# Banded and strided attention into a SoLU layer: local units of five and four blocks, masks seeded by ScalarE, w_out prepared with GpSimd and TensorE, and a new instruction order

## The chip, the cores and the metric

The kernel runs on one core of one Trainium2 chip, in one launch. The time is the device time of a whole execution in microseconds (us). The host only lays the data out.

## The reference

Eight batches, eight heads, 576 positions, head dimension 64. Four heads attend locally (a position sees itself and the 31 before it), four attend with stride 32 (the earlier positions with the same residue). Their outputs, side by side, are 4608 tokens of 512 values, which go through a SoLU layer with a layer norm.

```python
rel = pos[:, None] - pos[None, :]
mask_local = (rel >= 0) & (rel < 32)
mask_strided = (rel >= 0) & (pos[None, :] % 32 == pos[:, None] % 32)
attn = softmax(where(mask, q @ k.T / sqrt(64), -1e9)) @ v      # 4 local heads, 4 strided heads
x = attn_out.transpose(0, 2, 1, 3).reshape(4608, 512)
h = x @ w_in                                                   # 512 -> 1024
solu = h * softmax(h)
ln = (solu - mean(solu)) / sqrt(var(solu) + 1e-6) * g_ln
out = ln @ w_out                                               # 1024 -> 512
```

The two weight matrices come as 64-bit floats, everything else as 32-bit floats.

## The kernel before, in words

**Precision by pairs.** The large products run in float16 with each operand as a high and a low part: hi = cast(x), lo = x - hi, and three matmuls hi*hi, hi*lo, lo*hi. ScalarE (ACT) makes hi, VectorE (DVE) makes lo. Before that the weights and v are scaled by a power of two that comes of their sum of squares (`pow2_scale`). QK runs in float32.

**Weights.** `decode` loads a quarter of w_in or w_out (128 x 1024 numbers of 64 bits), lets ScalarE turn the high words into float32 values (L603), and VectorE shift the low words (L606) and OR their top three bits in (L607). w_in is decoded into `cc_sb`, and TensorE's Gram matmuls (L620) give its sum of squares; `whi`, `wlo` (the tile `w`) are its halves. w_out is decoded into `obuf`; eight ScalarE squares (L639) give its column sums, weighted by g; `ohi` (L651) and `olo` (in `obuf`, L652) are its halves, scaled by g and the power of two (`gs`). The raw words lie in "rooms": pieces of `raw_sb`, and once the buffers of two c transposes. `raw_sb` also holds the working tiles of the SoLU layer and a second v buffer, so that a room is free only when the work in it is done. The last quarter of w_out uses the room of an earlier one.

**Attention units.** A batch is cut into five units, `UNITS`: strided with 6 and 5 blocks, local with 3, 3 and 3. `unit(n)` issues for each: the mask into the score bank `s_ps` (by identity matmuls L369 for the first six units, later as a ScalarE copy L361, called a seed), the QK matmuls on top (L374), the row maximum (L380), the exponentials, either one per block with the maximum as bias (L385, units in `BY_BLOCK`) or a VectorE subtraction and one large exponential (L390, L392), sums and reciprocals, the multiply by the reciprocal on GpSimd (L401, POOL), the halves of p (L409, L410), one DMA transpose p to pt (L412), the PV matmuls into the banks `x_ps` (L432 strided, L442 local), and the copies of x as halves into the rings `xl`, `xs` (L461, L462). The local v is also needed shifted by half a tile: three DMAs copy it into `ve` (L338).

**Token blocks.** `ff(n)` does one of 36 blocks of 128 tokens: two times 12 large matmuls, called g1 here (L505 to L507), into two of three banks `h_ps`; the maximum (L511), the exponentials (L515), h times e (L517), the centring (L521), the square pass (L522), the powers on GpSimd, the halves of the result c (L562, L563), one DMA transpose of 16 tiles, cc to cc (L566), two times 12 large matmuls, called g2 (L575 to L577), into `o_ps`, and the scaled store (L583) with its DMA from ScalarE's queue.

**Order.** `Plan.add` records each step with its engine, a duration and its reads and writes; `ORDER` is a list of step numbers, and the program is issued in that order. Each engine works through its own steps in order. SP issues all loads and transposes from one queue, in order.

Of the kernel before, what the change touches and what calls it, by code (L numbers as in the profile page):

```python
# [753 lines left out]
```

## Time and profile before

| | us |
|---|---|
| median of three runs | 501.76 (500.56 to 502.09) |
| profiled execution | 501.38 |
| its span, first to last instruction | 499.7 |
| TensorE busy in the span | 462.6 (93%) |
| ScalarE / VectorE / GpSimd busy | 363.3 / 352.0 / 159.8 |
| mean granted TensorE clock | 0.952 |

A profile line names engine, operation, output and input tiles; "idle before" is the time in which the engine had nothing to do just before an instruction, with what ended it. PE is TensorE's matmul side and PEld its weight loads, which overlap. A clock of 0.5 is half of TensorE's full speed. The DMA share is the mean share of time in which a DMA engine was at work, added up over packets, so it can pass 1. In 40 slices of the span TensorE reads:

```profile
PE   6441889999999999999999999999999999999996
```

### The profile page before, as it was taken

How to read it: one execution, taken by the hardware profiler on the slowest of the kernel's cores; microseconds unless marked ns; L12 is line 12 of the kernel's file. 1: busy time of each engine (PE TensorE's matmuls, PEld its weight loads, DVE VectorE, ACT ScalarE, POOL GpSimd, SP SyncE). 2: the span in 40 equal slices, each digit the busy share in tenths (PEclk: the TensorE clock that was granted, in tenths of full speed). 3: DMA queues.
4: the chain of work that ended last, by engine and by line, in shares of the span. 5: the costliest groups of instructions: out<-in, count | busy, mean ns of one | idle time of the engine just before them, and what ended most of it. 6: DMA issues, size and time to landing. Idle time of an engine off the chain costs nothing.

```text
span 499.7 us, 12461 instructions
## 1 busy us (share of the span) xinstructions
PE 462.6 (93%) x5049; PEld 241.4 (48%) x5049; DVE 352.0 (70%) x740; ACT 363.3 (73%) x647; POOL 159.8 (32%) x312
## 2 busy tenths in 40 slices
PE   6441889999999999999999999999999999999996
PEld 5341544455455555555555545454555544444442
DVE  2988879678788777787877778578868664543440
ACT  3796899998687777888859667966857558455741
POOL 3210131662336163253442303450543304023220
PEclk8555889999999999999999999999999999999999
DMA  8999968599897599769969999449376465643343
GB/s 330 336 326 261 353 187 163 158 189 184 187 207 180 133 259 257 131 173 231 213 145 197 254 185 175 84 90 218 85 138 121 78 123 101 132 102 74 84 97 106
DMA packets 153818, 88.03 MB, mean 176 GB/s; under 512 B 139808, under 2 KB 140448, under 8 KB 153248
## 3 DMA queue, kind: packets, MB, share of 16 engines
q1 hardware_dynamic: 148576, 77.79, 69.8%
q10 hardware_dynamic: 5184, 9.44, 5.6%
q8 instruction: 39, 0.64, 0.5%
q14 instruction: 19, 0.16, 0.1%
HBM read 39.24 MB, written 9.44 MB: 97 GB/s over the span
## 4 chain that ended last, share of the span: by engine, by line
PE 80%; DMA 13%; ACT 3%; SPq 2%; DVE 1%; issue 1%; ACTq 0%; DVEq 0%
PE h_ps L505 11%; PE o_ps L575 11%; PE h_ps L507 11%; PE h_ps L506 11%; PE o_ps L576 11%; PE o_ps L577 11%; PE s_ps L374 6%; DMA raw<-w_in 4%; DMA cc<-cc 3%; DMA raw<-w_out 3%; PE x_ps L442 3%; DMA pt<-p 3%; PE x_ps L432 2%; DMA q<-qstr 1%; ACT t L385 1%
## 5 line engine op out<-in xcount | busy, mean ns | idle before, releaser
L575 PE MATMUL o_ps<-ohi,cc 128*128 128x512 f16 x272 | 103.3, 380 | 0.2
L577 PE MATMUL o_ps<-ohi,cc 128*128 128x512 f16 x272 | 103.1, 379 | 0.0
L576 PE MATMUL o_ps<-obuf,cc 128*128 128x512 f16 x272 | 103.1, 379 | 0.0
L401 POOL TENSOR_TENSOR t<-t,m 128x576 f32<-128x576 f32 (+2 forms) x40 | 48.5, 1214 | 117.3 <-DVE m L398 93.8
L511 DVE TENSOR_REDUCE st<-h_ps 128x1 f32<-128x512 f32 x70 | 47.3, 681 | 32.6 <-PE h_ps L507 32.3
L563 DVE SCALAR_TENSOR_TENSOR cc<-raw,st,cc 128x1024 f16<-128x1024 f32 (+1 forms) x38 | 46.6, 1229 | 23.5 <-ACT cc L562 23.1
L515 ACT ACTIVATE raw<-h_ps,st,vsc 128x512 f32<-128x512 f32 x62 | 47.8, 773 | 19.7 <-DVE st L513 18.8
L505 PE MATMUL h_ps<-w,xl 128*128 128x512 f16 x140 | 53.7, 384 | 1.8 <-DVE raw L517 1.8
L517 DVE SCALAR_TENSOR_TENSOR raw<-h_ps,raw 128x512 f32<-128x512 f32 x70 | 47.1, 683 | 11.7 <-ACT raw L515 11.2
L374 PE MATMUL s_ps<-k,q 64*54 64x54 f32 (+1 forms) x1280 | 45.6, 284 | 9.1 <-ACT s_ps L361 7.4
L507 PE MATMUL h_ps<-w,xl 128*128 128x512 f16 x140 | 53.6, 383 | 0.0
L506 PE MATMUL h_ps<-w,xl 128*128 128x512 f16 x140 | 53.6, 383 | 0.0
L505 PE MATMUL h_ps<-w,xs 128*128 128x512 f16 x140 | 53.5, 382 | 0.0
L521 ACT ACTIVATE raw<-raw,st 128x1024 f32<-128x1024 f32 x36 | 41.3, 1147 | 16.8 <-DVE st L520 15.8
L506 PE MATMUL h_ps<-w,xs 128*128 128x512 f16 x140 | 53.3, 381 | 0.0
L507 PE MATMUL h_ps<-w,xs 128*128 128x512 f16 x140 | 53.3, 381 | 0.0
L562 ACT ACTIVATE cc<-raw,st 128x1024 f16<-128x1024 f32 (+1 forms) x38 | 41.5, 1100 | 13.9 <-POOL st L552 9.6
L374 PEld LDWEIGHTS s_ps<-k,q 64*54 64x54 f32 (+1 forms) x1280 | 40.0, 201 | 19.8 <-ACT s_ps L361 8.8
L380 DVE TENSOR_REDUCE m<-s_ps 128x6 f32<-128x576 f32 (+2 forms) x40 | 30.4, 760 | 25.7 <-PE s_ps L374 25.2
L577 PEld LDWEIGHTS <-cc 128*128 128x128 f16 x288 | 28.2, 98 | 34.5 <-DMA cc<-cc 0.6
L575 PEld LDWEIGHTS <-cc 128*128 128x128 f16 x288 | 28.1, 98 | 33.4 <-DMA cc<-cc 1.0
L576 PEld LDWEIGHTS <-cc 128*128 128x128 f16 x288 | 28.2, 98 | 31.5
(149 smaller groups left out, 828.4 us busy)
## 6 DMA issues: line engine op xcount, KB each, us to landing
out<-ob ACTq DMA_DIRECT2D x36, 256.0 KB, 2.4
k<-kstr SPq DMA_DIRECT2D x8, 594.0 KB, 5.4
q<-qstr SPq DMA_DIRECT2D x8, 594.0 KB, 5.5
k<-kloc SPq DMA_DIRECT2D x8, 576.0 KB, 5.7
q<-qloc SPq DMA_DIRECT2D x8, 576.0 KB, 6.4
raw<-w_in SPq DMA_DIRECT2D x4, 1024.0 KB, 15.6
vrs<-vstr SPq DMA_DIRECT2D x5, 768.0 KB, 7.6
vrl<-vloc SPq DMA_DIRECT2D x5, 640.0 KB, 6.5
```

Of the source, the lines that this page charges most:

```text
L374: nc.tensor.matmul(s_ps[row : row + nq, pair, i * nk : (i + 1) * nk], q_raw[half][hs, q0 : q0 + (nq - 1) * nqb + 1 : nqb], k_raw[half][hs, ...
L401: add("pool", nx * nk / 520 + 0.03, lambda: nc.gpsimd.tensor_tensor(tv, tv, sm.unsqueeze(2).broadcast_to([P, nx, nk]), op=ALU.mult), r=TM, ...
L505: nc.tensor.matmul(hv[i], xhi[cc], whi[:, cc, cols], start=(cc == 0), stop=False)
L506: nc.tensor.matmul(hv[i], xhi[cc], wlo[:, cc, cols], start=False, stop=False)
L507: nc.tensor.matmul(hv[i], xlo[cc], whi[:, cc, cols], start=False, stop=(cc == 3))
L511: add("dve", 0.69, lambda i=i: nc.vector.tensor_reduce((nm, nm2)[i], hv[i], axis=AX.X, op=ALU.max, negate=True), r=[HH[i]], w=[(ST, "nm", i)])
L515: add("act", 0.73, lambda i=i, q=q: nc.scalar.activation(e[:, parts2[i]], hv[i], AF.Exp, bias=nm, scale=hs, accum_out=q), r=[HH[i], (ST, " ...
L517: add("dve", 0.7, lambda i=i, x=x: nc.vector.scalar_tensor_tensor(u[:, parts2[i]], hv[i], 1.0, e[:, parts2[i]], op0=ALU.mult, op1=ALU.mult ...
L563: add("dve", w / 980 + 0.23, lambda cols=cols: nc.vector.scalar_tensor_tensor(c[:, 1, cols], u[:, cols], r, c[:, 0, cols], op0=ALU.mult, o ...
L575: nc.tensor.matmul(o, ct[:, cc, :], ohi[:, cc, :], start=(cc == 0), stop=False)
L576: nc.tensor.matmul(o, ct[:, cc, :], olo[:, cc, :], start=False, stop=False)
L577: nc.tensor.matmul(o, ct[:, 8 + cc, :], ohi[:, cc, :], start=False, stop=(cc == 7))
```

## The change

- **Units.** `LATER` cuts batches 1 to 7 into four units: strided 6 and 5, local 5 and 4. Batch 0 keeps five. A local unit of more than four blocks puts its two head pairs in the two x banks, and its copies of x are two; one of four blocks or fewer uses one bank. The tiles t, p and pt are now bound to the unit's place in the batch, with transposes of 20 and 16 tiles.
- **Masks.** All units are seeded by ScalarE; the strided mask is read straight from the loaded masks. To make that possible TensorE's warm-up matmuls write the score banks once.
- **Weights.** The low word's top bits are taken by GpSimd from the highest byte of each low word, (byte - 15.5)/32 written as an integer; VectorE keeps only the OR. The squares of w_out are Gram matmuls; the scale is made of the sum of squares of w_out times that of g.
- **v.** The scrap output of v's squares goes into a buffer of vs instead of one of its own.
- **Order.** `ORDER` is another list throughout.

```diff
-BY_BLOCK = (2, 3, 4, 7, 8, 9)
+LATER = [(1, 0, 6), (1, 6, 5), (0, 0, 5), (0, 5, 4)]
+BY_BLOCK = (2, 3, 4, 7, 8)
 ORDER = """
-1 5 7 2 0 6 8 11 10 13 12 15 14 17 9 21 3 25 4 29 53 45 54 55 68 56 46 57 69 47 58 70 59 48 71 49 88 60 72 83 73 61 51 74 89 62 90 84 18 91 52 22 100
+1 6 2 15 3 16 4 14 11 13 19 20 25 18 53 30 52 54 17 35 60 12 55 56 10 58 5 61 144 92 59 21 22 62 123 63 9 76 23 64 77 27 65 24 66 78 67 79 93 97 80 68
 ...
-    def warm():
-        for _ in range(40):
-            nc.tensor.matmul(o_ps[:, 0:P], ones, ones, start=True, stop=True)
+    def warm(n, out):
+        for i in range(n):
+            nc.tensor.matmul(out[i % len(out)], ones, ones[:, 0:1].broadcast_to([P, 5 * KL]), start=True, stop=True)
 ...
     # unit(n)
-        half, b0, nb = UNITS[j]
+        half, b0, nb = (LATER if b else UNITS)[j]
-        if n >= SEEDED:
-            def seed():
-                nc.scalar.copy(s_ps[:, :, 0 : nb * nk], mk.unsqueeze(1).broadcast_to([P, 2, nb * nk]))
-            add("act", nx * nk / 1200 + 0.17, seed, r=["mask"], w=[("s", 0), ("s", 1)])
+        add("act", nx * nk / 1200 + 0.17, lambda: nc.scalar.copy(sv, mk), r=[MK], w=[("s", 0), ("s", 1)])
-            for pair, h, hs, row in heads if n < SEEDED else ():
-                nc.tensor.matmul(s_ps[row : row + D, pair, 0 : nb * nk], unit_sb[hs, hs], mk[hs], start=True, stop=False)
-        nt = 12
+        nt = 12 if half else 2 * nx
-        X = [("x", xb)] if half == 0 else [("x", 0), ("x", 1)]
+        one = half == 0 and nb <= 4
+        X = [("x", xb)] if one else [("x", 0), ("x", 1)]
 ...
     # v_scale(b)
-                nc.scalar.activation(junk[:, 0 : VW[a]], vr_sb[raw][a], AF.Square, scale=2.0**-SQ, accum_out=vm[:, a : a + 1])
+                nc.scalar.activation(junk[:, a, 0 : VW[a]], vr_sb[raw][a], AF.Square, scale=2.0**-SQ, accum_out=vm[:, a : a + 1])
 ...
     # decode
-            nc.vector.tensor_scalar(w0, w0, 29, None, op0=ALU.logical_shift_right)
-            nc.vector.scalar_tensor_tensor(di, di, 3, w0, op0=ALU.logical_shift_left, op1=ALU.bitwise_or)
+        top = raw.bitcast(U8).rearrange("p f (t b) -> p f t b", b=4)[:, :, 0, 3]
+        add("pool", 1.05, lambda: nc.gpsimd.tensor_scalar(w0, top, -15.5, 1.0 / 32, op0=ALU.add, op1=ALU.mult), r=RAW, w=[("low", n)])
+        add("dve", 1.25, lambda: nc.vector.scalar_tensor_tensor(di, di, 3, w0, op0=ALU.logical_shift_left, op1=ALU.bitwise_or),
 ...
     # prep_o
-            for cc in (2 * i, 2 * i + 1):
-                add("act", 0.71, lambda cc=cc: nc.scalar.activation(ob_sb[cc % 2][:, 0 : DM // 2].bitcast(BF16), obuf[:, cc], AF.Square,
-                                                                   scale=2.0**-SQ, accum_out=o_sc[:, 8 + cc : 9 + cc]),
+            def gram(i=i, dst=dst):
+                x = dst.bitcast(BF16).rearrange("p (f t) -> p f t", t=2)[:, :, 1]
+                for j in range(8):
+                    nc.tensor.matmul(o_ps[:, 0:P], x[:, j * P : j * P + P], x[:, j * P : j * P + P], start=(i == 0 and j == 0), stop=(i == 3 and j == 7))
+            add("pe", 0.6, gram, r=OD, w=["o"])
```

The order moves everywhere; three places show what. The names are those of the tiles above, with a buffer number.

SP's queue around the loads of w_out, before (two quarters have the room `raw`, one the room in `cc`; the last of the four is the third `raw<-w_out`):

```order
L285 DMA raw_67<-w_out 128x2x1024
L412 DMA_TRANSPOSE pt_98<-p_94 128x12x128
L338 DMA ve_74<-vl_71 32x2x1024
L338 DMA ve_74<-vl_71 64x2560
L285 DMA raw_67<-w_out 128x2x1024
L661 DMA g_118<-g 128x8
L412 DMA_TRANSPOSE pt_97<-p_96 128x12x128
L285 DMA cc_103<-w_out 128x2x1024
L285 DMA k_65<-kloc 128x1152
L285 DMA raw_67<-w_out 128x2x1024
L285 DMA q_63<-qloc 128x1152
```

The same place now:

```order
L288 DMA raw_67<-w_out 128x2x1024
L411 DMA_TRANSPOSE pt_97<-p_95 128x12x128
L288 DMA k_66<-kstr 128x1188
L342 DMA ve_73<-vl_70 64x2560
L288 DMA raw_67<-w_out 128x2x1024
L288 DMA cc_102<-w_out 128x2x1024
L411 DMA_TRANSPOSE pt_96<-p_94 128x12x128
L288 DMA raw_67<-w_out 128x2x1024
L288 DMA k_65<-kloc 128x1152
L288 DMA q_63<-qloc 128x1152
```

The last quarter now stands ahead of both local loads of batch 1; the strided k of batch 1 and one copy into ve stand ahead of the second quarter.

ScalarE from the decode of the last quarter to the first square pass of a token block, before (L639 are the squares of w_out, L515 the exponentials of block 0, L325 the split of the next v):

```order
L603 ACTIVATE obuf_114<-raw_67 128x1024
L639 ACTIVATE ob_105,o_sc_117<-obuf_114 128x512
L409 CAST p_96<-t_86 128x12x54
L392 ACTIVATE t_87<-t_87 128x540
L639 ACTIVATE ob_104,o_sc_117<-obuf_114 128x512
L639 ACTIVATE ob_105,o_sc_117<-obuf_114 128x512
L639 ACTIVATE ob_104,o_sc_117<-obuf_114 128x512
L515 ACTIVATE raw_67,st_106<-h_ps,st_106,vsc_77 128x512
L461 CAST xl_99<-x_ps 128x2x192
L515 ACTIVATE raw_67,st_106<-h_ps,st_106,vsc_77 128x512
L325 ACTIVATE vl_71<-vrl_69,vsc_78 128x1280
L409 CAST p_94<-t_87 128x2x5x54
```

The same place now, to the centring (the square pass L520 comes next):

```order
L601 ACTIVATE obuf_113<-raw_67 128x1024
L408 CAST p_94<-t_85 128x6x96
L364 CAST s_ps<-mk_loc_81 128x2x480
L391 ACTIVATE t_84<-t_84 128x540
L408 CAST p_92<-t_83 128x12x54
L384 ACTIVATE t_85,m_89<-s_ps,m_89 128x96 x10
L459 CAST xl_98<-x_ps 128x2x192
L513 ACTIVATE raw_67,st_105<-h_ps,st_105,vsc_76 128x512 x2
L652 ACTIVATE ohi_109<-obuf_113,gs_118 128x512 x2
L408 CAST p_93<-t_84 128x2x5x54
L519 ACTIVATE raw_67<-raw_67,st_105 128x1024
```

The squares are gone, the v split comes later, and the ten block exponentials of the first five-block unit stand ahead of the exponentials of block 0.

TensorE at the first output-layer matmul, before (84 of the g1 matmuls stand ahead of it, and the QK of a local unit directly):

```order
L507 LDWEIGHTS xs_102
L507 MATMUL h_ps<-w_113,xs_102 128x512
L374 MATMUL s_ps<-k_65,q_63 64x96 x12
L575 LDWEIGHTS cc_103
L575 MATMUL o_ps<-ohi_110,cc_103 128x512
```

And now:

```order
L505 MATMUL h_ps<-w_112,xs_101 128x512
L263 LDWEIGHTS ones_111
L263 MATMUL s_ps<-vm_74,ones_111 128x1
L263 LDWEIGHTS ones_111
L263 MATMUL s_ps<-vm_74,ones_111 128x1
L573 LDWEIGHTS cc_102
L573 MATMUL o_ps<-ohi_109,cc_102 128x512
```

Again 84 g1 matmuls stand ahead (a float32 QK matmul counts twice in the profile); the QK of the four-block unit and one PV of 60 matmuls of batch 1 now come behind.

More of the change, by code (lines that the diff above doesn't have):

```diff
@@ L262, in total @@
             for i, part in enumerate(parts):
-                nc.tensor.matmul(tot, ones, part.bitcast(BF16)[:, 1:2], start=(i == 0 and not adds), stop=(i == len(parts) - 1), skip_group_check=adds)
+                one = product or not (i or adds)
+                nc.tensor.matmul(tot[:, i : i + 1] if product else tot, ones, part.bitcast(BF16)[:, 1:2], start=one, stop=product or i == len(parts) - 1, skip_group_check=adds)
         add("pe", 0.06 * len(parts) + 0.05, total, r=["ones", *r], w=[T])
         def root():
-            nc.vector.tensor_scalar(dst[:, 0:1].bitcast(I32), tot.bitcast(I32), 1, 0x7F800000, op0=ALU.logical_shift_right, op1=ALU.bitwise_and)
+            low = tot
+            if product:
+                low = dst[:, 0:1]
+                nc.vector.tensor_scalar(low, tot[:, 0:1], tot[:, 1:2], None, op0=ALU.mult)
+            nc.vector.tensor_scalar(dst[:, 0:1].bitcast(I32), low.bitcast(I32), 1, 0x7F800000, op0=ALU.logical_shift_right, op1=ALU.bitwise_and)
         def fn():
@@ L300, in v_scale @@
         raw = raw_v(b)
+        junk = v_sb[1][b % 2]
         for a in range(2):
             def square(a=a):
-                nc.scalar.activation(junk[:, 0 : VW[a]], vr_sb[raw][a], AF.Square, scale=2.0**-SQ, accum_out=vm[:, a : a + 1])
-            add("act", (1.36, 1.58)[a], square, r=[("vr", a, raw)], w=["junk", ("vm", b % 2, a)])
+                nc.scalar.activation(junk[:, a, 0 : VW[a]], vr_sb[raw][a], AF.Square, scale=2.0**-SQ, accum_out=vm[:, a : a + 1])
+            add("act", (1.36, 1.58)[a], square, r=[("vr", a, raw)], w=[("v", 1, b % 2, a), ("vm", b % 2, a)])
         room = (s_ps[:, 1, 512 - b : 513 - b], ("s", 1)) if b else (h_ps[2][:, 0:1], ("h", 2))
-        pow2_scale(sc, [vm[:, 0:1], vm[:, 1:2]], [("vm", b % 2, a) for a in range(2)], ("vsc", b % 4), room, 8, 1.0 / P_SCALE, adds=b > 1)
+        pow2_scale(sc, [vm[:, 0:1], vm[:, 1:2]], [("vm", b % 2, a) for a in range(2)], ("vsc", b % 4), room, 8, 1.0 / P_SCALE, adds=b > 0)
         def hscale():
@@ L374, in qk @@
                     nc.tensor.matmul(s_ps[row : row + nq, pair, i * nk : (i + 1) * nk], q_raw[half][hs, q0 : q0 + (nq - 1) * nqb + 1 : nqb],
-                                     k_raw[half][hs, k0 : k0 + nk], start=False, stop=(i == nb - 1), skip_group_check=n >= SEEDED)
-        add("pe", nb * 0.231 + (0.25, 0.09)[half] - (0.2 if n >= SEEDED else 0.0), qk, r=[("q", half), ("k", half), "mask", "unit", "kpad"], w=[("s", 0), ("s", 1)])
+                                     k_raw[half][hs, k0 : k0 + nk], start=False, stop=(i == nb - 1), skip_group_check=True)
+        add("pe", nb * 0.231 + (0.25, 0.09)[half] - 0.2, qk, r=[("q", half), ("k", half), "kpad"], w=[("s", 0), ("s", 1)])
         SS = [("s", 0), ("s", 1)]
@@ L404, in unit @@
         if half == 0:
-            hi, lo = (pb[:, 6 * a : 6 * a + 6, 0:nk] for a in range(2))
+            hi, lo = (pb[:, nx * a : nx * a + nx, 0:nk] for a in range(2))
         else:
@@ L449, in unit @@
             q0, w = off + QL * b0, QL * nb
-            src = [x_ps[xb][:, 0 : 2 * w].rearrange("p (c q) -> p c q", c=2)]
-            dst = [[x[:, :, q0 : q0 + w] for x in xl]]
+            src = [x_ps[xb][:, 0 : 2 * w].rearrange("p (c q) -> p c q", c=2)] if one else [x[:, 0:w] for x in x_ps]
+            dst = [[x[:, :, q0 : q0 + w] for x in xl]] if one else [[x[:, c, q0 : q0 + w] for x in xl] for c in range(2)]
             ring = [("xl", q0 // QL + i) for i in range(nb)]
@@ L458, in unit @@
         for c, (src, (dh, dl)) in enumerate(zip(src, dst)):
-            w = 2 * by_row[c] * nq if half else nx * nq
-            K = [(*x, c) if half else x for x in ring]
+            w = 2 * by_row[c] * nq if half else (2 if one else 1) * nb * nq
+            K = [(*x, y) for x in ring for y in (range(2) if one else (c,))]
             add("act", w / 1200 + 0.17, lambda src=src, dh=dh: nc.scalar.copy(dh, src), r=[X[c]], w=[(*x, "h") for x in K])
@@ L479, in ff @@
         bs = sorted({n * P // S, (n * P + P - 1) // S})
-        ring = [("xl", pos // QL + i, a) for i in range(2) for a in "hl"]
+        ring = [("xl", pos // QL + i, c, a) for i in range(2) for c in range(2) for a in "hl"]
         ring += [("xs", b % 2, b0, c, a) for b in bs for b0 in R0 for c in range(2) for a in "hl"]
@@ L673, in attn_solu_kernel @@
         v_split(b, 0)
-        for j in range(2, NU - 1):
+        last = len(LATER if b else UNITS) - 1
+        for j in range(2, last):
             unit(b * NU + j)
@@ L681, in attn_solu_kernel @@
                 o_factor(b + 1)
-        unit(b * NU + NU - 1)
+        unit(b * NU + last)
         if b == 0:
```

85 lines of the change are left out of this document (41 added, 44 removed), and 82 rows, old and new, of the table ORDER.

## The prediction

> **What bounds the kernel now.** I read the page's totals and clock row, then busy time by stretches of the span, then the chain of waits around the stretch that is not full, then ScalarE and TensorE there in order of time.
>
> ```profile
> PE 462.6 (93%) x5049; PEld 241.4 (48%) x5049; DVE 352.0 (70%) x740; ACT 363.3 (73%) x647; POOL 159.8 (32%) x312
> PEclk8555889999999999999999999999999999999999
> ...
> 22.00:53.00 31.00, 13.32 (x360) 11.58 (x361) 26.92 (x51) 22.99 (x53) 4.06 (x4) 0.50 1.10 286
> 53.00:82.00 29.00, 24.91 (x309) 12.32 (x308) 24.93 (x53) 27.09 (x62) 4.83 (x5) 0.93 0.86 228
> ...
> 0.00:82.00 82.00, 49.38 (x862) 33.21 (x863) 64.38 (x127) 63.51 (x137) 15.48 (x26) 0.71 0.97 287
> 82.00:475.00 393.00, 392.30 (x4097) 199.06 (x4094) 282.14 (x603) 291.92 (x498) 141.25 (x277) 1.00 0.74 158
> 475.00:499.70 24.70, 20.91 (x97) 9.12 (x94) 5.48 (x12) 7.89 (x13) 3.09 (x9) 1.00 0.41 101
> ```
>
> The columns are the length, then busy time of PE, PEld, DVE, ACT, POOL, then clock and DMA share. From 82 to 475 us TensorE idles 393.00 - 392.30 = 0.70 us: nothing another engine saves there is worth more. It idles 3.79 us at the end and 32.62 us before 82, where its clock is 0.71 on average. So the time is "when the queue of TensorE fills" plus the work behind that point. I anchor on the first output-layer matmul (L575): 84 first-layer matmuls (g1) stand ahead of it in the old order, and 84 in the new.
>
> ```profile
> 26.58 2.03 ACT t L385 x12
> ...
> 40.73 6.84 DMA raw<-w_out
> ...
> 48.81 1.23 DVE obuf L607
> 50.07 7.03 DMA raw<-w_out
> ```
>
> This is the chain of waits: the second quarter of w_out lands at 47.57 and is decoded, its OR ends at 50.04, that frees the room for the last quarter, which is issued at 50.07 and lands at 57.10. ScalarE, which had idled 4.43 us for the second quarter, then runs without a pause:
>
> ```profile
> 47.60 1.19 ACT L603 ACTIVATE obuf<-raw 128x1024 f32<-128x1024 f32 x1 [4.43 <-DMA raw<-w_out]
> ...
> 52.35 0.68 ACT L409 CAST p<-t 128x576 f16<-128x576 f32 x1
> 52.92 0.63 ACT L639 ACTIVATE ob<-obuf 128x512 bf16<-128x512 f32 x1
> ...
> 55.56 0.64 ACT L361 CAST s_ps<-mk_loc 128x576 f32<-128x576 bf16 x1
> 57.12 1.20 ACT L603 ACTIVATE obuf<-raw 128x1024 f32<-128x1024 f32 x1 [0.93 <-DMA raw<-w_out]
> ...
> 60.60 0.63 ACT L639 ACTIVATE ob<-obuf 128x512 bf16<-128x512 f32 x1
> ...
> 61.21 0.62 ACT L639 ACTIVATE ob<-obuf 128x512 bf16<-128x512 f32 x1
> ...
> 63.76 1.36 ACT L325 ACTIVATE vl<-vrl,vsc 128x1280 f16<-128x1280 f32 x1
> 65.01 0.63 ACT L409 CAST p<-t 128x540 f16<-128x540 f32 x1
> ...
> 69.71 1.35 ACT L651 ACTIVATE ohi<-obuf,gs 128x512 f16<-128x512 f32 x2
> 70.93 1.07 ACT L522 ACTIVATE raw<-raw 128x1024 f32<-128x1024 f32 x1
> ...
> 71.97 0.79 ACT L515 ACTIVATE raw<-h_ps,st,vsc 128x512 f32<-128x512 f32 x1
> ```
>
> The decode of the last quarter starts at 57.12 and the square pass of token block 0 (L522) is over at 71.97: 14.85 us. TensorE over the same time:
>
> ```profile
> 52.83 0.61 PE L505 MATMUL h_ps<-w,xl 128*128 128x512 f16 x1
> 61.82 0.28 PE L442 MATMUL x_ps<-pt,ve 96*64 96x64 f16 x6 [2.23 <-DMA pt<-p]
> 64.31 0.63 PE L505 MATMUL h_ps<-w,xl 128*128 128x512 f16 x1
> 64.74 0.63 PE L506 MATMUL h_ps<-w,xl 128*128 128x512 f16 x1
> ...
> 67.53 0.38 PE L507 MATMUL h_ps<-w,xs 128*128 128x512 f16 x1
> 77.14 0.75 PE L432 MATMUL x_ps<-pt,vs 54*64 54x54 f16 x60
> 78.41 0.38 PE L505 MATMUL h_ps<-w,xl 128*128 128x512 f16 x1 [0.52 <-DVE raw L517]
> 81.97 0.39 PE L575 MATMUL o_ps<-ohi,cc 128*128 128x512 f16 x1
> 82.19 0.38 PE L576 MATMUL o_ps<-obuf,cc 128*128 128x512 f16 x1
> ```
>
> The anchor is 81.97, ten us after L522 is over (GpSimd's powers, the split of c, its transpose). A matmul leaves every 0.22 us there, and every 0.43 us from 64.31 to about 67.5, after the 2.23 us of idling before 61.82.
>
> **The change, part by part.**
>
> *Low weight bits by GpSimd.* VectorE loses eight shifts and keeps the eight ORs:
>
> ```profile
> L606 DVE TENSOR_SCALAR raw<-raw 128x1024 int32<-128x1024 int32 x7 | 4.8, 691 | 1.4 <-DMA raw<-w_out 1.4
> L401 POOL TENSOR_TENSOR t<-t,m 128x576 f32<-128x576 f32 x4 | 4.6, 1146 | 31.5 <-DVE m L398 31.5
> L231 POOL CAST mk_str<-mask 128x324 bf16<-128x324 f32 x1 | 0.5, 452 | 1.1 <-DMA mask<-masks 1.1
> L232 POOL CAST mk_loc<-mask 128x96 bf16<-128x96 f32 x1 | 0.3, 267 | 0.0
> ```
>
> That is 8 x 0.69 = 5.5 us off VectorE, which is busy 26.92 of 31 us in 22 to 53. GpSimd gets eight one-input passes over 1024 elements, of a form the trace does not have (bytes in, int32 out). The two casts give (452 - 267)/228 = 0.81 ns an element, 1.02 us for 1024; the two-input multiply gives 1146 x 1024/576 = 2.04 us. I take 1.05, near the casts, since it has one input. GpSimd is idle 27 of the 31 us and the pass runs beside ScalarE's decode (1.08 us slot, 57.12 to 58.20), so up to 1.1 us it costs nothing; at 2.04 each decode ends 0.9 us later, and two decodes in a row lie on the path of the last quarter: +1.8 us.
> [...]
>
> *Squares of w_out by TensorE.* Eight ScalarE squares go, 0.61 us each start to start (60.60, 61.21), 4.9 us; 32 small matmuls take their place on an engine that is idle 17.7 us in 22 to 53. The column scale now comes of one sum and one multiply; nothing waits longer for that than it did for the squares.
>
> *Masks by ScalarE.* The first six units lose their identity matmuls on TensorE, which waits there anyway (0 gained), and each gets a ScalarE seed of the kind at 55.56: about 0.6 us, 3.6 us in all. ScalarE is busy 22.99 of 31 us in 22 to 53, so the seeds fill pauses like the 4.43 us before 47.60; they eat most of what the squares leave.
>
> *Loads.* In the new SP order the last w_out quarter stands ahead of the two local q/k loads of batch 1, and its room is freed by the decode of the second quarter as before. That second quarter was issued at 40.73. In the new queue it stands behind the transpose of the second local unit, whose p is ready after some 11 us of ScalarE work (two six-block exponentials of 2.03, two squares of v, four casts, a decode) from the first local exponentials at about 23.5; then come 0.9 MB of k and ve. I put the issue at 38 and the landing seven us later, at 45 in place of 47.57, so the last issue moves from 50.07 to about 47. With the 7.03 us to landing it would be there at 54; the 0.59 MB of k ahead of it is gone (2 us at 286 GB/s, of which I count a third). I take 53.3 for the decode. Bounds: 49 (ScalarE's own work of 22 to 53, 22.99 + 3.6 of seeds less three squares, 24.8 us, from 24 on) and 57.1 (no change, as the DMA share of 1.10 allows).
>
> *ScalarE from that decode to the end of L522.* Against the 14.85 us: four squares go (4 x 0.61 = 2.45), the split of vl goes behind (63.76 to 65.01: 1.25), two of four scalings L651 go behind (69.71 to 70.93: 1.22); in come one cast of 576 (52.35 to 52.92: 0.57), a seed of 960 elements (0.64 for 576, 1.07 if all of that scales; I take 0.9) and four more block exponentials (the five-block unit has ten; six took 2.03 at 26.58, so 1.35). Sum 14.85 - 4.92 + 2.82 = 12.75 us. The old stretch had no wait in it; the new one must wait for g1 of block 0, whose second half TensorE starts only after the last gram: I add 1.3 us (0 to 2.5). L522 is over at 53.3 + 14.05 = 67.3, and the anchor, ten us later, at 77.3: 4.7 us earlier.
>
> *What TensorE has not yet done there.* In the new order one PV of 60 matmuls (0.75 us, at 77.14) and one of six local QK blocks come behind the anchor. A three-block QK takes 0.89 us:
>
> ```profile
> 219.96 0.89 PE s_ps L374 x24
> 220.84 0.69 PE x_ps L442 x36
> 221.53 0.32 PE h_ps L505
> ```
>
> so a block is 0.30 us: +1.05 us.
>
> *Units of 5 and 4 blocks after batch 0.* The number of matmuls is the same, and so are the transposed tiles (36 a batch). Attention stands between the large matmuls 37 times behind the anchor, 43 before. Each return costs 0.32 - 0.22 = 0.10 us (221.53 against the spacing): -0.6 us; bounds 0 and -1.5. Per batch one seed, one exponential, a handful of VectorE passes with their fixed cost and one transpose issue go; the scrap output of v's squares moves into a half of vs that no PV reads any more. In 82 to 475 all that is hidden under TensorE, so 0. What hides them is that TensorE's queue always has a large matmul ready; a unit that is late uncovers them (rival 3).
>
> *New pauses behind the anchor.* 0.70 us now. A new order on the same bookkeeping will have some of its own; I put +1.0 us, bounds -0.7 and +4.
>
> Sum: -4.7 + 1.05 - 0.6 + 1.0 = -3.2 us. The profiled execution took 501.38 us (span 499.7), 0.4 under the median of 501.76; 501.38 - 3.2 = 498.2.
>
> **Rivals.**
> 1. *The last quarter lands as late as before.* For it: DMA share 1.10 in 22 to 53, so moving loads only moves the queue; four transposes and the same megabytes stand ahead of it. Against: SP idled on an OR at 50.07, not on bytes. L522 is then over at 57.1 + 14.0 = 71.1, the anchor at 81.1, and the sum is -0.9 + 1.45 = +0.5: 501.9.
> 2. *The clock falls again.* Block 3's g1 needs the bank that block 1's exponential frees, which ScalarE now runs behind block 0's c: TensorE may idle about 2 us shortly before the anchor. The 2.23 us before 61.82 cost 3.4 us at 0.43 in place of 0.22 us a matmul, 1.7 us; pauses of 0.52 us (78.41) did not. 499.9, or 500.9 with a longer pause. [...]
> 3. *Slower: the five-block unit comes late.* Its PV writes both x banks and needs one transpose of 20 tiles, so ScalarE and VectorE must have emptied both banks and the whole unit must have gone through GpSimd. Price: a PV that waits for its transpose,
>
> ```profile
> PE x_ps L442 <- DMA pt<-p: 2.7, 2, 2.2
> ```
>
> 1.35 us on average. In all seven units that is +9.5, 507.7; in half of them 503. It ends slower from 0.46 us a unit (3.2/7) on. Against: GpSimd and ScalarE have 150 and 100 us spare in 82 to 475.
> 4. *More.* The quarter lands when ScalarE gets there (50.5): anchor 74.5, 495.4.
>
> **How the numbers follow.** Forecast 0.52, rival 1 0.13, rival 2 0.11, rival 3 0.11, rival 4 0.13. A change under 0.3% (1.5 us, about what this kernel's measurement can tell from none) comes of rival 1, of half of rival 2 and of the weak end of the forecast: 0.22. Slower: rival 3 and a little of rival 1, 0.12. Faster: 0.66. The range leaves out the bad end of rival 3 and the far end of rival 4: 495.0 to 501.9; the forecast alone is 496.5 to 500.
>
> **What would show it.** The first output-layer matmul near 77 (72 to 74: rival 4; 80 and later: rival 1); the last w_out landing near 53; GpSimd's 1024-element passes near 1.05 us; no ScalarE pause of 4 us before a w_out decode; clock 1.0 from about 58 on; TensorE's idle time from the anchor to 475 under 2 us. The prediction is wrong if that idle time is several us, with a releaser "DMA pt<-p" or ScalarE's x copies ahead of a PV, or if g1 starts later than 52.83.

## The result, and the profile after

The changed kernel takes 504.39 us (median of 5 runs, 503.48 to 504.94), the kernel before, timed with it, 502.09 us (500.56 to 502.41): ratio 1.0058, 95% interval 1.0036 to 1.0079. Slower by 0.6%, where I had forecast 498.2. The profiled execution has a span of 501.8 us (before 499.7) and took 503.48, so the traces show 2.1 us of the loss.

The page's clock row and the busy times by stretch, as shown of before (length, busy time of PE, PEld, DVE, ACT, POOL, clock, DMA share, GB/s):

```profile
PEclk8555699999999999999999999999999999999999
...
22.00:53.00 31.00, 13.43 (x330) 11.28 (x324) 25.31 (x40) 24.31 (x62) 10.71 (x10) 0.50 1.02 259
53.00:82.00 29.00, 26.51 (x326) 14.35 (x326) 24.92 (x59) 24.34 (x55) 7.21 (x7) 0.89 0.85 251
82.00:475.00 393.00, 390.74 (x4160) 199.82 (x4159) 286.37 (x566) 289.69 (x475) 137.51 (x270) 1.00 0.71 157
475.00:501.80 26.80, 21.91 (x100) 9.26 (x97) 5.02 (x11) 8.21 (x14) 3.11 (x9) 1.00 0.43 98
```

TensorE is busier from 53 to 82 (26.51 against 24.91) and idles 2.26 us from 82 to 475 (before 0.70) and 4.89 behind 475 (before 3.79). ScalarE in order of time, the decodes of w_out (L601), the pass that ends in the square (L520), and what it waited for:

```profile
39.12 1.14 ACT L601 ACTIVATE obuf<-raw 128x1024 f32<-128x1024 f32 x1 [0.92 <-DMA raw<-w_out]
48.27 1.12 ACT L601 ACTIVATE obuf<-raw 128x1024 f32<-128x1024 f32 x1 [3.19 <-DMA raw<-w_out]
51.44 1.15 ACT L601 ACTIVATE obuf<-cc 128x1024 f32<-128x1024 f32 x1 [0.69 <-DMA cc<-w_out]
56.28 1.13 ACT L601 ACTIVATE obuf<-raw 128x1024 f32<-128x1024 f32 x1 [1.44 <-DMA raw<-w_out]
61.70 0.73 ACT L408 CAST p<-t 128x648 f16<-128x648 f32 x1 [2.28 <-POOL t L400]
63.08 0.34 ACT L384 ACTIVATE t<-s_ps,m 128x96 f32<-128x96 f32 x1 [0.64 <-DVE m L386]
71.16 1.06 ACT L520 ACTIVATE raw<-raw 128x1024 f32<-128x1024 f32 x1
```

The second quarter is decoded at 48.27 (before 47.60), the last at 56.28 (57.12), and the square pass is over at 72.21 (71.97). TensorE, with its pauses:

```profile
50.82 1.89 PE L643 MATMUL o_ps<-obuf 128*128 128x128 bf16 x16 [3.06 <-DVE obuf L607]
53.16 0.37 PE L440 MATMUL x_ps<-pt,ve 96*64 96x64 f16 x6 [0.45 <-DVE xs L460]
55.49 0.61 PE L503 MATMUL h_ps<-w,xl 128*128 128x512 f16 x1
55.89 0.63 PE L504 MATMUL h_ps<-w,xl 128*128 128x512 f16 x1
...
60.11 1.43 PE L373 MATMUL s_ps<-k,q 64*64 64x96 f32 x40
...
69.11 0.38 PE L503 MATMUL h_ps<-w,xl 128*128 128x512 f16 x1 [0.54 <-DVE raw L515]
77.01 0.38 PE L503 MATMUL h_ps<-w,xl 128*128 128x512 f16 x1 [1.70 <-DVE raw L515]
82.26 0.38 PE L573 MATMUL o_ps<-ohi,cc 128*128 128x512 f16 x1
...
95.46 0.38 PE L573 MATMUL o_ps<-ohi,cc 128*128 128x512 f16 x1 [1.35 <-POOL st L523]
...
485.65 0.38 PE L575 MATMUL s_ps<-ohi,cc 128*128 128x512 f16 x1
486.16 0.39 PE L573 MATMUL o_ps<-ohi,cc 128*128 128x512 f16 x1
492.24 0.39 PE L573 MATMUL h_ps<-ohi,cc 128*128 128x512 f16 x1 [0.72 <-DMA cc<-cc]
495.27 0.39 PE L573 MATMUL h_ps<-ohi,cc 128*128 128x512 f16 x1 [0.27 <-DMA cc<-cc]
```

The first output-layer matmul, my anchor, stands at 82.26 (before 81.97; forecast 77.3). Behind it the span has 419.54 us left, 417.73 before. So of the 2.1 us, 0.3 lie ahead of the anchor and 1.8 behind. I had put -4.7 and +1.45. The miss is nearly all ahead of the anchor.

### The profile page after: what moved, and what is told of

It reads as the page before. It is cut to its first block, busy times and chain, and to the rows that moved or that the text cites. A ratio compares the mean times of both kernels' runs of the same rounds, so it can differ in the third digit from the quotient of the medians.

```text
span 501.8 us, 12292 instructions
## 1 busy us (share of the span) xinstructions
PE 461.3 (92%) x5023; PEld 240.2 (48%) x5023; DVE 352.3 (70%) x695; ACT 360.2 (72%) x617; POOL 166.6 (33%) x312
## 4 chain that ended last, share of the span: by engine, by line
PE 80%; DMA 9%; ACT 7%; DVE 2%; issue 1%; SPq 1%; POOL 0%; DVEq 0%; ACTq 0%
PE o_ps L573 11%; PE h_ps L503 11%; PE o_ps L575 11%; PE o_ps L574 11%; PE h_ps L504 11%; PE h_ps L505 11%; PE s_ps L373 7%; PE x_ps L440 3%; DMA q<-qloc 3%; DMA cc<-w_out 2%; DMA cc<-cc 2%; PE x_ps L430 2%; DMA raw<-w_out 1%; DMA k<-kstr 1%; ACT t L384 1%; ACT ohi L652 1%
## 5 line engine op out<-in xcount | busy, mean ns | idle before, releaser
L515 DVE SCALAR_TENSOR_TENSOR raw<-h_ps,raw 128x512 f32<-128x512 f32 x70 | 47.4, 682 | 25.9 <-ACT raw L513 25.2
L373 PE MATMUL s_ps<-k,q 64*54 64x54 f32 (+1 forms) x1280 | 44.0, 285 | 21.9 <-ACT s_ps L364 15.9
L400 POOL TENSOR_TENSOR t<-t,m 128x648 f32<-128x648 f32 (+4 forms) x33 | 46.6, 1412 | 50.1 <-DVE m L397 25.6
L548 POOL TENSOR_SCALAR st<-st 128x1 f32<-128x1 f32 x32 | 7.4, 230 | 147.6 <-ACT raw L520 141.3
L504 PE MATMUL h_ps<-w,xs 128*128 128x512 f16 x140 | 53.3, 381 | 0.0
L505 PE MATMUL h_ps<-w,xs 128*128 128x512 f16 x140 | 53.3, 381 | 0.0
L373 PEld LDWEIGHTS s_ps<-k,q 64*54 64x54 f32 (+1 forms) x1280 | 38.8, 201 | 29.9 <-ACT s_ps L364 18.6
L560 ACT ACTIVATE cc<-raw,st 128x1024 f16<-128x1024 f32 (+1 forms) x38 | 41.7, 1101 | 15.3 <-POOL st L550 10.3
L573 PEld LDWEIGHTS <-cc 128*128 128x128 f16 x288 | 28.1, 98 | 36.3 <-DMA cc<-cc 2.6
L575 PEld LDWEIGHTS <-cc 128*128 128x128 f16 x288 | 28.2, 98 | 34.0
L581 ACT ACTIVATE ob<-o_ps,st 128x512 f32<-128x512 f32 x34 | 23.3, 686 | 28.2 <-PE o_ps L575 10.3
```

What stands on the lines that cost most here:

```text
L373: nc.tensor.matmul(s_ps[row : row + nq, pair, i * nk : (i + 1) * nk], q_raw[half][hs, q0 : q0 + (nq - 1) * nqb + 1 : nqb], k_raw[half][hs, ...
L400: add("pool", nx * nk / 520 + 0.03, lambda: nc.gpsimd.tensor_tensor(tv, tv, sm.unsqueeze(2).broadcast_to([P, nx, nk]), op=ALU.mult), r=TM, ...
L504: nc.tensor.matmul(hv[i], xhi[cc], wlo[:, cc, cols], start=False, stop=False)
L505: nc.tensor.matmul(hv[i], xlo[cc], whi[:, cc, cols], start=False, stop=(cc == 3))
L515: add("dve", 0.7, lambda i=i, x=x: nc.vector.scalar_tensor_tensor(u[:, parts2[i]], hv[i], 1.0, e[:, parts2[i]], op0=ALU.mult, op1=ALU.mult ...
L573: nc.tensor.matmul(o, ct[:, cc, :], ohi[:, cc, :], start=(cc == 0), stop=False)
```

## The experiments

Times are medians, ratios are to the kernel before, timed on the same chip in the same session (its medians: 501.58, 500.98, 501.27 and 501.79 us), taken over the whole session, so that they need not be the quotient of two medians. Of each version one execution has a profile. A name with b_ is an edit of the kernel before, the others of the changed one. A row of numbers in a diff is a piece of ORDER.

### Does the last w_out quarter set the anchor?

own_room:

```diff
-            decode(dst, src, 4 + i, OD, (ROOMS[2], ROOMS[3], LAST_ROOM, ROOMS[2])[i], W_SHIFT)
+            decode(dst, src, 4 + i, OD, (ROOMS[2], ROOMS[3], LAST_ROOM, ROOMS[0])[i], W_SHIFT)
-153 155 106 45 90  ...  149 160 305 304 275
+153 155 106 160 45 90  ...  149 305 304 275
```

> The changed kernel, but the last quarter of w_out is loaded into the room of the first w_in quarter, free since about 25 us, and its load is issued right behind the transpose that stood ahead of it, near 45 us in place of 50.8. Theory A (the last quarter no longer sets when the output layer starts: TensorE's 84 g1 ahead of it and ScalarE's row of work between 57 and 82 do): the quarter lands 3 to 4 us earlier, its decode moves from 56.3 to about 54, the first output-layer matmul stays at 81.5 to 82.5, the time within 0.7 us of the changed kernel's 504.4. Theory B (my prediction's: decode of the last quarter plus 14 us plus 10 us is the start of the output layer): start 2 us earlier or more, time 502 to 502.5.

504.23 us, 1.0055 (1.0036 to 1.0074): no gain. ScalarE, then TensorE:

```profile
47.05 1.12 ACT L601 ACTIVATE obuf<-raw 128x1024 f32<-128x1024 f32 x1 [3.92 <-DMA raw<-w_out]
...
53.65 1.15 ACT L601 ACTIVATE obuf<-raw 128x1024 f32<-128x1024 f32 x1
55.42 0.67 ACT L408 CAST p<-t 128x576 f16<-128x576 f32 x1 [0.61 <-POOL t L400]
60.13 0.73 ACT L408 CAST p<-t 128x648 f16<-128x648 f32 x1 [2.43 <-POOL t L400]
61.84 0.34 ACT L384 ACTIVATE t<-s_ps,m 128x96 f32<-128x96 f32 x1 [0.98 <-DVE m L386]
...
81.00 0.38 PE L573 MATMUL o_ps<-ohi,cc 128*128 128x512 f16 x1
```

The last quarter is decoded at 53.65, where I had forecast it (53.3), without a wait. But the waits behind it grew from 2.92 to 4.02 us, and the anchor is at 81.00, not 77.3. It is 33.95 us behind the decode of the *second* quarter; in the changed kernel 82.26 - 48.27 = 33.99. The 1.3 us by which it is earlier go with the second quarter of this execution (47.05, 1.2 us earlier), and the median shows none of it. By its time theory A holds.

b_room_tail puts the same question to the kernel before, where ScalarE has no pause behind that decode:

```diff
-                   (ROOMS[2], ROOMS[3], LAST_ROOM, ROOMS[2])[i])
+                   (ROOMS[2], ROOMS[3], LAST_ROOM, ROOMS[0])[i])
 (SP: the last w_out load right behind the third, local q behind local k;
  transpose of block 33's c ahead of the four of block 34's)
```

> The kernel before with the last w_out quarter in the room of the first w_in quarter, issued right behind the third (45 us in place of 50.1), the local q load behind it, and block 33's transpose ahead of block 34's. Theory A (the last quarter's decode sets the start in the kernel before, whose ScalarE has no pause behind it: my reading of its profile): decode at 54 to 55.5 in place of 57.1, start 1 to 2.5 us earlier, with 0.3 to 0.5 of the tail 498.5 to 500.3 against 501.5. Theory B (as own_room in the changed kernel: pauses only move): the tail's 0.5 at most, 501 to 501.6.

503.64 us, 1.0040 (1.0020 to 1.0060): slower, as neither theory had it. The decode moved from 57.12 to 55.66 and the anchor from 81.97 to 81.84: TensorE waits 2.29 us at 73.21 instead, and its matmuls then leave every 0.43 us up to about 77 (before has such a spell from 64.31 on, which this profile lacks). So the anchor is where theory B has it, but one profile cannot tell how much of that is the clock. The tail lost: waits of 0.69 and 1.05 us for "DMA cc<-cc" at 481.93 and 485.31, where before has none. The transpose that helps the changed kernel (below) holds up block 34 here.

### The loads

small_loads loads a quarter of the bytes of the first two w_out quarters, to see what own_room left open. Three eighths of w_out are then missing from its result; the instructions are the same:

```diff
-        load(2.61, room, src, RAW, [("pt", 1)] if n == 4 else [])
+        if n in (4, 5):
+            dst_part = room.rearrange("p a f -> p (a f)")[:, 0:512]
+            src_part = src[:, 0, 0:512]
+            load(2.61, dst_part, src_part, RAW, [("pt", 1)] if n == 4 else [])
+        else:
+            load(2.61, room, src, RAW, [])
```

> The changed kernel with three quarters of the first and of the second w_out load left out (1.57 MB less to read between 32 and 48 us; the weights there are then not w_out's, the instructions on all engines are the same). Theory (the row starts with the second quarter's landing, and the output layer stands 34.0 us behind its decode, as in the changed kernel, 48.27 to 82.26, and in own_room, 47.05 to 81.00): decode near 45, start near 79, time 501 to 502.5. Rival (the loads only fill ScalarE's and TensorE's waits): start within 1 us of 82, time 503.7 to 504.6.

501.95 us, 1.0015 (0.9992 to 1.0038): 0.43% less than the changed kernel's 1.0058 (the two intervals just overlap). Second decode and anchor:

```profile
45.23 1.15 ACT L606 ACTIVATE obuf<-raw 128x1024 f32<-128x1024 f32 x1 [1.26 <-DMA raw<-w_out]
...
50.59 0.37 PE L440 MATMUL x_ps<-pt,ve 96*64 96x64 f16 x6 [0.91 <-DMA pt<-p]
...
79.78 0.38 PE L573 MATMUL o_ps<-ohi,cc 128*128 128x512 f16 x1
```

The first row is ScalarE's, the others TensorE's. 3.0 us earlier at the decode, 2.5 at the anchor, and the anchor is 34.55 us behind the decode (33.99 in the changed kernel). So bytes taken out of the first two quarters' loads do move the anchor, where an earlier last quarter did not. What hands this on to TensorE is not separated: the second quarter, the third (decoded at 47.81, in the changed kernel at 51.44) and the transpose for which the PV ahead of the first g1 waits here stand one behind the other in SP's queue, and all three come earlier.

### TensorE's clock

kept_clock:

```diff
     # unit(n), at the end of qk()
+            if n == 4:
+                warm(22, [o_ps[:, 0 : 5 * KL]])
 ...
     # prep_o, in gram(), ahead of its matmuls
+                if i == 0:
+                    warm(12, [o_ps[:, 0 : 5 * KL]])
```

> The changed kernel plus 34 matmuls whose result nobody reads, in two pauses of TensorE: 22 behind the local QK block at 36.6 us (the pause of 7.3 us) and 12 ahead of the first w_out gram (the pause of 3.1 us). Theory A (half clock on the first twelve g1, one QK and one PV costs about 2.9 us of TensorE at the place where the whole queue stands): g1 spaced 0.22 us from its first on in place of 0.43, QK of the five-block unit 2.5 us earlier (57.5), its exponentials too, output layer 1 to 2.5 us earlier, time 502 to 503.4. Rival (ScalarE's row sets the start; TensorE only waits longer elsewhere): clock as said, the start at 81.8 to 82.3, time 504 to 504.8. Slower by about 1 if the fillers run at half clock throughout and hold up the PV behind them.

505.31 us, 1.0069 (1.0047 to 1.0091): no gain. TensorE:

```profile
37.82 6.10 PE L221 MATMUL o_ps<-ones 128*128 128x480 bf16 x22
...
57.36 0.39 PE L505 MATMUL h_ps<-w,xl 128*128 128x512 f16 x1
57.58 0.38 PE L506 MATMUL h_ps<-w,xl 128*128 128x512 f16 x1
...
62.86 0.37 PE L373 MATMUL s_ps<-k,q 64*64 64x96 f32 x4 [2.62 <-DMA q<-qloc]
```

The first g1 runs at 0.22 us a matmul, as meant, and then the QK behind it waits 2.62 us for the local q of batch 1. That load stands on SP behind the last w_out quarter (issues at 50.79 and 51.73 in the changed kernel): the new order of loads, which I had counted as a gain of some 0.7 us, has this price once TensorE gets there earlier. The profiles of tail and dve_bits, with the changed kernel's loads, have the wait too, 1.27 and 1.19 us. In this profile the second quarter also came late (50.41), so the anchor is at 85.19; whether the idle matmuls slow the loads cannot be told from this one.

room_clock_tail joins the edits of own_room, kept_clock and tail; room_tail is the same without the idle matmuls.

> The changed kernel with three edits at once: the last w_out quarter in the room of the first w_in quarter (as in own_room), the 34 idle matmuls (as in kept_clock), the transpose of block 33 ahead of block 34's (as in tail). Theory (in kept_clock the first g1 ran at full clock, but the QK behind them then waited 2.62 us for the local q of batch 1, whose load stands on SP's queue behind the last w_out quarter; with that quarter issued early the load goes out at about 47 us, so the wait is gone): no wait of that QK, output layer from 79 to 80.5 us, 2 us of gain of the clock and 1.5 of the tail, time 500.5 to 501.5. Rival (the clock buys nothing, ScalarE's row sets the start in any case): start at 81 to 82.3, 502.5 to 503.2, the tail's gain alone.

501.57 us, 1.0004 (0.9985 to 1.0023): level with the kernel before, 0.54% below the changed one. The time is close to the theory's, the path is not: the QK still waits 0.99 us for q at 60.53, and the anchor is at 82.65 where 79 to 80.5 was expected (in this profile the second quarter came at 49.70).

> room_clock_tail without the 34 idle matmuls. Theory (the first g1 at half clock cost about 1.2 us of the 2.7 that room_clock_tail gained on the changed kernel, the tail 1.5): ratio to before 1.002 to 1.004, 502.3 to 503.2. Rival (the room for the last quarter and with it the earlier q and k loads brought it, the clock nothing): ratio 0.999 to 1.002.

503.01 us, 1.0027 (1.0007 to 1.0047), as tail alone (1.0029). From the second decode to the anchor it takes 34.73 us, room_clock_tail 32.95. So with q there earlier the clock seems to bring 0.23%, 1.2 us. The two intervals overlap, so that the times do not show it; the profiles, one of each, differ the same way by 1.78 us.

b_kept_clock, the same in the kernel before, in the pause of 2.23 us on which my rival 2 was priced:

```diff
+            if n == NU + 2:
+                for _ in range(10):
+                    nc.tensor.matmul(o_ps[:, 0:480], ones, ones[:, 0:1].broadcast_to([P, 480]), start=True, stop=True)
```

> The kernel before plus ten matmuls whose result nobody reads, behind the QK at 58.65 us, in TensorE's pause of 2.23 us. Theory (that pause drops the clock, and about ten g1 spaced 0.43 us in place of 0.22 cost 2.1 us on the path that sets the output layer): g1 at 0.22 us throughout, 1.3 to 2.1 us faster than before, 499.7 to 500.5 against 501.8. Rival (ScalarE's row sets the start): clock as said, time within 0.5 us.

500.87 us, 0.9998 (0.9985 to 1.0011): nothing. The pause and the half clock are gone (0.44 us is left, for q at 58.13; behind it the g1 leave 0.22 us apart), and another wait has grown, 0.68 us at 74.46 before:

```profile
59.01 2.22 PE L378 MATMUL o_ps<-ones 128*128 128x480 bf16 x10
...
73.14 0.38 PE L508 MATMUL h_ps<-w,xl 128*128 128x512 f16 x1 [1.56 <-DVE raw L520]
```

That wait, for VectorE's pass behind ScalarE's exponential, takes back 0.9 us. The anchor of this profile is still 1.58 us earlier (80.39), but from 82 to 475 us TensorE idles 1.84 us, where before idles 0.70: 0.37 for "DMA pt<-p" at 86.12 and 0.31 for "DMA cc<-cc" at 105.39 are among it.

### The tail

```diff
-1484 1481 1483 1441  ...  1442 1497 1503 1461 1500
+1484 1481 1461 1483 1441  ...  1442 1497 1503 1500
```

> The changed kernel with one transpose issue moved on SP's queue: that of block 33's c ahead of the four of block 34, instead of behind them (same work, 12 tiles and addresses as before). Theory (the three pauses of TensorE at 485.7, 491.1 and 494.6, 0.51 + 1.10 + 0.65 us in all less the 0.21 a matmul that they include, hang on that transpose, since c of block 35 writes the buffer that it reads): c of the last block starts 2 us earlier, all three pauses go, time 1.2 to 1.9 us less than the changed kernel: 502.5 to 503.2. Rival (the last pauses are the time of the chain of block 35 itself, exponentials, powers, split, transpose): first pause gone, the others stay, 0.3 us less or nothing.

502.95 us, 1.0029 (1.0009 to 1.0049), 0.29% less than the changed kernel. The two intervals overlap, but room_tail stands 0.28% below own_room in the same way. From 480 us on TensorE has no wait left in the profile, and the span behind the anchor is 417.70 us, 1.8 less (room_tail 418.45). As by the theory.

### The parts one by one

dve_bits undoes GpSimd's low bits (its edit is shown), b_bits adds them to the kernel before:

```diff
-        add("pool", 1.05, lambda: nc.gpsimd.tensor_scalar(w0, top, -15.5, 1.0 / 32, op0=ALU.add, op1=ALU.mult), r=RAW, w=[("low", n)])
-        add("dve", 1.25, lambda: nc.vector.scalar_tensor_tensor(di, di, 3, w0, op0=ALU.logical_shift_left, op1=ALU.bitwise_or),
+        add("pool", 0.01, lambda: None, r=RAW, w=[("low", n)])
+
+        def bits():
+            nc.vector.tensor_scalar(w0, w0, 29, None, op0=ALU.logical_shift_right)
+            nc.vector.scalar_tensor_tensor(di, di, 3, w0, op0=ALU.logical_shift_left, op1=ALU.bitwise_or)
+
+        add("dve", 2.02, bits,
```

> The changed kernel with the low weight bits back on VectorE: shift and OR one behind the other, 0.69 us more of VectorE for each of eight quarters, GpSimd's eight passes (1.1 to 1.8 us each) gone. Theory A (VectorE is full between 22 and 60 us, and the OR waits for GpSimd only where a multiply stands ahead of it): slower by 0.5 to 1.5 us, 505 to 506. Rival (GpSimd's pass is later than ScalarE's decode and slows VectorE beside it, 24.02 us: 1.8 us a pass): no change or up to 0.7 us faster, 503.7 to 504.6.

504.86 us, 1.0056 (1.0024 to 1.0088).

> The kernel before with one part of the change: low weight bits by GpSimd, in its old order (each pass of GpSimd stands beside ScalarE's decode). Theory (VectorE is full between 22 and 60 us, and the chain of waits runs through two ORs of it): 0.5 to 1.5 us faster, 500.3 to 501.3 against 501.8. Rival (as in dve_bits, where the opposite edit changed nothing that could be measured): within 0.5 us.

501.29 us, 1.0009 (0.9990 to 1.0028). In neither kernel is a difference measured between the two engines.

b_squares and b_seeds add the sums on TensorE and the ScalarE seeds to the kernel before; act_squares undoes the sums in the changed one:

```diff
     # b_squares
-            for cc in (2 * i, 2 * i + 1):
-                add("act", 0.71, lambda cc=cc: nc.scalar.activation(ob_sb[cc % 2][:, 0 : DM // 2].bitcast(BF16), obuf[:, cc], AF.Square,
 ...
+        add("dve", 0.2001, lambda: nc.vector.scalar_tensor_tensor(gs_sb, g_sb, 1.0, g_sb, op0=ALU.mult, op1=ALU.mult, accum_out=o_sc[:, 9:10]), r=["g"], w=["gm", "gs"])
 ...
+            add("pe", 0.6001, gram, r=OD, w=["o"])
 ...
     # b_seeds
-SEEDED = NU + 1
+SEEDED = 0
```

> The kernel before with one part of the change: squares of w_out by 32 small matmuls of TensorE in place of eight ScalarE squares, otherwise in its old order. Theory A (my prediction's: ScalarE from the decode of the last quarter on sets the start of the output layer, and four squares of 0.61 us go out of that stretch): output layer 2 us earlier or more, 499.5 to 500.3. Theory B (the row of TensorE sets it: the sums now stand on its queue among the g1, waiting for VectorE's ORs): no gain, 501.8 to 504.

507.77 us, 1.0129 (1.0100 to 1.0158). One row of VectorE, one of ScalarE, then TensorE:

```profile
47.37 0.17 DVE L639 SCALAR_TENSOR_TENSOR gs<-g 128x8 f32<-128x8 f32 x1 [7.90 <-DMA g<-g]
...
52.40 0.61 ACT L366 CAST s_ps<-mk_str 128x540 f32<-128x540 bf16 x1 [4.13 <-DVE t L395]
...
53.06 1.30 PE L379 MATMUL s_ps<-k,q 64*54 64x54 f32 x40 [11.60 <-ACT s_ps L366]
55.78 1.03 PE L649 MATMUL o_ps<-obuf 128*128 128x128 bf16 x8 [1.42 <-DVE obuf L612]
...
57.85 1.03 PE L649 MATMUL o_ps<-obuf 128*128 128x128 bf16 x8
```

The first g1 starts at 59.92 in place of 52.83, the anchor is at 88.36. The first two sums stand in TensorE's queue behind the QK: 1.42 us of waiting for VectorE's OR and about one us each, some 3.4 of the 7.1 us. So theory B's wait is there. The other 3.7 us come by the QK itself (53.06 in place of 49.34), from another step of the edit: g's sum of squares stands in VectorE's queue ahead of the second quarter's OR and waits 7.90 us for the load of g, and the seed, behind VectorE's work, comes that much later. In the changed kernel the same step is done at 10.3. So b_squares does not price the sums alone.

> The kernel before with one part of the change: masks of the first six units copied into PSUM by ScalarE instead of added by identity matmuls, otherwise in its old order. Theory (3.6 us more for ScalarE, which waits 4.4 us for the second w_out quarter anyway): 0 to 1 us slower, 501.8 to 502.8. Rival (a seed stands on ScalarE's queue behind decodes that wait for a load, so QK and everything behind it comes later): 1 to 3 us slower.

500.87 us, 0.9989 (0.9970 to 1.0007): nothing, as I had costed it.

> The changed kernel with one part undone: the squares of w_out by ScalarE again (eight passes of 0.6 us, put where they cost least), the 32 small matmuls gone, the rest in the changed order. Theory A (in the changed order ScalarE's row from 57 us on does bear on the start, so that the squares' 4.9 us did bring something there, which other work in the new order used up: the ten block exponentials of 3.3 us stand ahead of block 0's): 1.5 to 3 us slower, 506 to 507.4. Theory B (TensorE's row alone sets it): within 0.5 us, 504 to 504.9.

505.49 us, 1.0100 (1.0078 to 1.0122), by the ratios 2.1 us above the changed kernel (1.0036 to 1.0079, so that the intervals just touch; the two were timed in different sessions). So in the new order the sums seem to bring about what I had put down for ScalarE, 2.45. The profile does not isolate it: its anchor is 1.70 us later, but TensorE pauses 2.22 us at 70.50 there and runs at 0.43 us a matmul for 3.3 us behind it (71.88 to 75.20), which is worth about as much (last section).

### Another order

reordered is room_clock_tail with the steps of 20 to 130 us in another order, reordered_nofill the same without the idle matmuls.

> The kernel of room_clock_tail (own room for the last quarter, idle matmuls, block 33's transpose first) with the steps between 20 and 130 us put in another order: looked for with a replay in which loads share 265 to 295 GB/s and the clock is full from 47 us on. Same instructions. Theory (what remains is order: copies that stand behind a decode which waits for a load, and the ten block exponentials ahead of block 0's): output layer at 77.5 to 79.5 us, more attention done ahead of it, 496 to 498.5. Rival (the replay's loads are too orderly; the next load is late instead): 500 to 502, as room_clock_tail.

512.07 us, 1.0226 (1.0195 to 1.0257).

> As reordered, without the 34 idle matmuls. Theory (half clock on the first g1 costs what it cost in the changed kernel): 1.5 to 2.5 us slower than reordered. Rival (the idle matmuls hold up the work behind them as much as they bring): the same as reordered.

511.06 us, 1.0200 (1.0164 to 1.0235). Both some ten us slower than room_clock_tail, against both theories of reordered. Between the two no difference is measured, as the rival of reordered_nofill has it. In reordered the first g1 comes at 59.16, the anchor at 85.00, and 424.5 us lie behind it, 7 more than in room_clock_tail. From the anchor to 475 us TensorE idles 4.46 us (4.80 from 82 on, less 0.34 just ahead of the anchor), where room_clock_tail idles 1.69 from 82 on; 1.44 us at 99.87 and 0.45 at 116.22 are waits for "DMA cc<-cc". That is 2.8 of the 7; the rest fits the attention that was not done ahead of the anchor (230 matmul records from 53 to 82 us against 334). Why the replay had put the anchor some six us earlier is not settled. No version here is shown to beat the kernel before.

## Why the prediction was wrong, step by step

| kernel | second decode | first g1 | anchor | second decode to anchor | first g1 to anchor | span behind the anchor |
|---|---|---|---|---|---|---|
| before | 47.60 | 52.83 | 81.97 | 34.37 | 29.14 | 417.73 |
| changed | 48.27 | 55.49 | 82.26 | 33.99 | 26.77 | 419.54 |
| own_room | 47.05 | 54.26 | 81.00 | 33.95 | 26.74 | 419.60 |
| small_loads | 45.23 | 52.93 | 79.78 | 34.55 | 26.85 | 419.62 |
| act_squares | 48.26 | 56.25 | 83.96 | 35.70 | 27.71 | 419.54 |
| tail | 48.02 | 55.70 | 84.20 | 36.18 | 28.50 | 417.70 |
| room_tail | 49.52 | 57.54 | 84.25 | 34.73 | 26.71 | 418.45 |
| room_clock_tail | 49.70 | 56.66 | 82.65 | 32.95 | 25.99 | 417.25 |

In tail and act_squares the g1 leave 0.43 us apart a second time between the first g1 and the anchor (77.50 to 80.85 and 71.88 to 75.20; last section).

- **The step that failed** is the one from the decode of the last quarter to the end of L522 and to the anchor ten us behind it, taken as cause and effect. own_room decoded that quarter 2.6 us earlier and won no time; its anchor moved by 1.26 us, as did its second quarter (1.22). In the chain of before I took the last link, an issue at 50.07 behind an OR, for the one that decides; ScalarE's row had waits to give as well as work, and they only moved. What the rows show instead is an anchor about 34 us behind the second quarter, and 26.7 to 26.9 us behind the first g1 in the changed kernel, own_room, small_loads and room_tail; the loads ahead of these set it.
- **The first g1.** The prediction has no term for when TensorE can start it, though it named a start later than 52.83 as a sign of being wrong. It came at 55.49, 2.66 us later than before, and only 2.37 of that are won back up to the anchor. Ahead of it TensorE waits 3.06 us for the second quarter's OR and then for VectorE's copy of x (0.45) or, in small_loads, tail and room_tail, for the transpose of its PV (0.9). Which of these decides is open; the chain that ended last in the changed kernel's profile runs through the third quarter, landed at 51.42.
- **The loads.** I put the second quarter's issue at 38 and its landing at 45. It was issued at 39.69 and decoded at 48.27: k and ve, 0.9 MB, stand ahead of it, and the DMA share is 1.02 as it was 1.10. In my sum that late second quarter is the last quarter's decode at 56.28 for 53.3: 3.0 of the 5.0 us by which the anchor was missed. The words for it stood in rival 1 ("moving loads only moves the queue"); I gave it 0.13.
- **ScalarE's stretch**: 14.05 forecast, 15.93 measured. Its work was right (12.75 against 15.93 - 2.92 = 13.01), the waits were not: 2.92 for 1.3. This is 1.9 of the 5.0 us; the ten us behind L522 (L520 now) were right, 10.05. 2.28 us are for GpSimd's product for a unit ahead, 0.64 for the five-block unit, whose QK TensorE reached only at 60.11, the first ten g1 having run at 0.43 us.
- **Squares by TensorE**: -2.45 forecast, 2.1 measured when undone (act_squares, not isolated there). I had priced no wait of their own on TensorE's queue; b_squares shows one, and a larger one on VectorE's queue, where the order is not made for them. In the changed order the sums wait 3.06 us at 50.82, at a place where the next PV goes at 53.16; in act_squares, without the sums, it waits for its transpose until 53.24.
- **Low bits**: costed at nothing, and nothing was measured (dve_bits, b_bits). The pass is longer than the 1.05 I took:

```profile
L606 POOL TENSOR_SCALAR raw<-raw x7: 1107/1269/1986, 12.7 to 56.7; 128x1024 int32<-128x1024 uint8 x7
```

  The columns are the least, the median and the longest time in ns. It cost no time that can be measured. The median is 0.22 us above my 1.05, which I had estimated from the two casts; the longest comes near the 2.04 of the two-input multiply.
- **Seeds**: 0 forecast, none measured (b_seeds).
- **Behind the anchor**: +1.05 - 0.6 + 1.0 = +1.45 forecast, +1.81 measured. The pauses from 82 to 475 are +1.56 for +1.0 (waits of 0.59 at 89.90, 0.31 at 92.96 and 1.35 at 95.46; none later). The tail is +1.10, for which I had no term: a moved transpose issue, in the chain that ended last. So the remainder, work moved and fewer insertions, is -0.85 where I had +0.45.
- **Rivals.** Rival 1 came nearest (quarter as late as before, anchor 81.1, 501.9 for 503.48), by the same failed step, so its nearness is in part luck. Rival 3 did not happen: no wait for "DMA pt<-p" behind the anchor. (GpSimd's spare time there was 393.00 - 141.25 = 252 us, not 150.) Rival 2's pause of about two us is there, 1.70 at 77.01, at the place I had named; in this execution the matmuls behind it are 0.22 us apart (last section).

## What to carry to other kernels

When a chain of waits runs through several loads, it names the last one only because it was last; take each away in thought and see which wait ends next, and price a moved load by the bytes queued ahead of it. Work put on an in-order queue also puts its wait there: b_squares lost 6.5 us with an edit that takes eight passes off ScalarE, over half of it by one short VectorE step that waited 7.90 us for a load of 4 KB. And when the instruction order changes everywhere, the tail is part of the sum: one transpose issue was worth about 0.3%.
